# A second feed-forward layer by a seven-product form of Strassen's algorithm, in a kernel bound by TensorE

## The chip, the cores and the metric

The kernel runs on one core of a Trainium2 chip. The metric is the device time of one execution in microseconds, and lower is better. Each run of a kernel lies beside runs of the kernel before on the same chip.

## The reference

Attention with projected keys and values (64 rows for 1,024 tokens), followed by a two-layer feed-forward network. Cut to what matters:

```python
# q, k, v: [8, 8, 1024, 64]   E, F: [64, 1024]
k_proj = einsum('ks,bhsd->bhkd', E, k);  v_proj = einsum('ks,bhsd->bhkd', F, v)
scores = q @ k_proj.T / sqrt(64);        attn = exp(scores - max)
x      = (attn / attn.sum(-1)) @ v_proj          # -> [8192, 512]
h      = x @ w_in                                # w_in  [512, 2048]
g      = h * sigmoid(1.702 * h)
out    = g @ w_out                               # w_out [2048, 512]
```

## The kernel before

The 8,192 tokens are worked in 16 blocks of 512, two for each of eight batch rows. For each block TensorE does the first layer (64 matmuls of 512 columns) and the second (64 more). Attention work for later blocks (scores, values, sums of exponentials, projections of keys and values) is slipped in between groups of these matmuls, in slots. The order on each engine is fixed by the program.

TensorE's results go to PSUM, which the program uses as eight buffers; the kernel before splits them in two pools:

```python
ps_f = ctx.enter_context(tc.tile_pool(name="ps_f", bufs=4, space=PSUM))   # feed-forward layers, scores, projections
ps_x = ctx.enter_context(tc.tile_pool(name="ps_x", bufs=4, space=PSUM))   # values, sums
```

The second layer and the values with their normalization:

```python
def ffn2(j, n, fcs):                     # token tile n of block j
    ...
    if fcs.start == 0:
        o_ps[n] = f_tile([P, DM])
    for fc in fcs:
        nc.tensor.matmul(o_ps[n], gts[j][:, fc, n * P:(n + 1) * P], w_out_sb[:, fc, :],
                         start=(fc == 0), stop=(fc == FC - 1))
    ...

def sums(h):                             # row sums of exp, then their reciprocals
    ...
    for e in range(2):
        nc.vector.reciprocal(rden[:, e, :], d_ps[e])

def spread(h):                           # reciprocals to DRAM, and back to all partitions
    rdr = dram.tile([HP, 2, TB], F32, name="rdr")
    nc.sync.dma_start(out=rdr, in_=rdens.pop(h)[0:P:32])
    rbc[h] = att.tile([P, HP, TB], F32, name="rbc")
    for e, r in enumerate((LO, HI)):
        nc.sync.dma_start(out=rbc[h][r], in_=rdr[None, :, e, :].to_broadcast([D, HP, TB]))

def values(h, u):
    n_ps = [ps_x.tile([P, TB], F32, name="x_ps") for _ in range(2)]
    eight(n_ps, ...)                     # 8 matmuls per pair of heads
    for i in range(2):                   # waits for the broadcast reciprocals
        nc.vector.tensor_tensor(x_of(h)[:, 2 * u + i, :], n_ps[i], rbc[h][:, 2 * u + i, :], op=ALU.mult)

for b in range(4, B):                    # keys and values of row b; frees the buffers of the next row's loads
    at(2 * b - 4, O + 6, proj(b), kv_out(b))
for j in range(3, NBLK - 1):             # O + n: after part n of block j's second layer; conditions for the first and last blocks cut
    at(j, O + 6 * u, scores(j + 3, u))   # for u in 0, 1
    at(j, O, values(j + 1, 1))
    at(j, O, sums(j + 2), spread(j + 2))
    at(j, O + 6, values(j + 2, 0))
```

The softmax here doesn't subtract the row's maximum and nothing guards it: scores larger than these inputs give would overflow.

## Time and profile before

| | before |
|---|---|
| time, median of 4 runs | 508.68 us (508.45 to 509.11) |
| span of the profiled run | 508.2 us |
| TensorE busy | 501.5 us, 99% |
| VectorE busy | 155.0 us, 31% |

The lines of the profile that carry this are in the prediction below. A line of cost groups reads: source line, engine, operation, output <- inputs, count | busy us, mean ns of one | idle time of the engine just before them and what ended it. A line of the timeline reads: start, duration, engine, line, operation, and in brackets how long the engine had been idle and what it waited for. "SPq" and "POOL ... DMA" lines are issues of transfers.

### The profile page before, as it was taken

What the parts mean: (1) busy time and instruction counts of PE and PEld (TensorE: products, weight loads), DVE (VectorE), ACT (ScalarE), POOL (GpSimd) and SP (SyncE); (2) the same over time, 40 slices, a digit from 0 to 9 for tenths busy, and PEclk for the clock granted to TensorE, in tenths of its full rate; (3) what the DMA queues carried; (4) which work ended last, traced back from release to release, by engine and by line L of the source; (5) the groups of instructions that cost most, each with busy time, mean ns of one, the idle gap of its engine ahead of it and who ended that gap; (6) DMA issues with size and microseconds to landing.
All of it is one profiled execution on the core that took longest, in us unless ns stands there. A gap on an engine that the chain in (4) does not pass through costs nothing.

```text
span 508.2 us, 7066 instructions
## 1 busy us (share of the span) xinstructions
PE 501.5 (99%) x3018; PEld 227.7 (45%) x3018; DVE 155.0 (31%) x207; ACT 262.3 (52%) x427; POOL 80.4 (16%) x100
## 2 busy tenths in 40 slices
PE   7999999999999999999999999999999999999997
PEld 3644445444444444444444444444444444444444
DVE  4503204508151624216161331616224161611000
ACT  1665473655637365572746537374563737244351
POOL 6462250500510510041000510000000000000000
PEclk9999999999999999999999999999999999999999
DMA  9999999999899997599928989190603205050202
GB/s 166 200 190 207 201 152 175 219 215 126 150 211 267 134 230 128 159 131 101 234 47 212 99 121 236 29 227 1 173 0 79 88 8 160 1 166 1 83 1 83
DMA packets 127831, 68.76 MB, mean 135 GB/s; under 512 B 94724, under 2 KB 118660, under 8 KB 125880
## 3 DMA queue, kind: packets, MB, share of 16 engines
q0 software_dynamic: 86496, 29.37, 52.8%
q1 hardware_dynamic: 41224, 38.69, 31.3%
q8 instruction: 23, 0.38, 0.3%
q10 hardware_dynamic: 80, 0.26, 0.2%
q14 instruction: 8, 0.07, 0.0%
HBM read 72.88 MB, written 16.99 MB: 177 GB/s over the span
## 4 chain that ended last, share of the span: by engine, by line
PE 95%; DMA 3%; POOL 1%; DVE 0%; issue 0%; ACT 0%; POOLq 0%
PE f_ps L399 44%; PE f_ps L423 43%; DMA v_sb<-in_v_dram 3%; PE f_ps L169 3%; PE f_ps L258 2%; PE x_ps L258 1%; PE f_ps L415 1%; PE x_ps L296 1%; POOL k_sb L57 0%; POOL v_sb L57 0%; PE x_ps L371 0%; PE x_ps L386 0%; PE f_ps L239 0%; POOL q_even L96 0%; DVE x_sb L358 0%
## 5 line engine op out<-in xcount | busy, mean ns | idle before, releaser
L423 PE MATMUL f_ps<-w_out_sb,gT 128*128 128x512 bf16 x1008 | 226.7, 379 | 0.0
L399 PE MATMUL f_ps<-xT,w_in_sb 128*128 128x512 bf16 (+1 forms) x1032 | 224.3, 377 | 0.0
L401 ACT ACTIVATE gT<-f_ps 128x512 bf16<-128x512 f32 (+1 forms) x258 | 150.4, 594 | 58.4 <-PE f_ps L399 58.0
L399 PEld LDWEIGHTS <-w_in_sb 128*128 128x128 bf16 x1032 | 100.7, 98 | 119.7 <-issue 0.8
L423 PEld LDWEIGHTS <-gT 128*128 128x128 bf16 x1008 | 95.9, 98 | 121.8 <-issue 11.8
L426 ACT COPY o_sb<-f_ps 128x512 f32<-128x512 f32 x63 | 37.0, 587 | 130.7 <-PE f_ps L423 120.9
L331 DVE TENSOR_TENSOR xT<-x_ps,rbc 128x512 bf16<-128x512 f32 x52 | 33.3, 684 | 219.2 <-PE x_ps L258 117.8
L299 DVE RECIPROCAL rden<-x_ps 128x512 f32<-128x512 f32 x26 | 85.3, 3322 | 16.2 <-PE x_ps L296 16.1
L69 POOL DMA_DIRECT2D q_sb<-in_q_dram x48 | 42.1, 901 | 153.3 <-DMA qT<-q_sb 124.1
L277 ACT ACTIVATE expT<-f_ps 128x512 bf16<-128x512 f32 (+1 forms) x54 | 28.5, 580 | 29.4 <-PE f_ps L258 29.3
L277 ACT ACT_TABLE_LOAD x13 | 16.7, 1283 | 4.7 <-PE f_ps L258 4.5
L281 ACT ACT_TABLE_LOAD x14 | 18.0, 1283 | 0.2
L57 POOL DMA_DIRECT2D k_sb<-in_k_dram x10 | 8.5, 847 | 48.0 <-PE f_ps L169 41.9
L169 PE MATMUL f_ps<-k_sb,eft 128*64 128x512 bf16 x56 | 13.4, 382 | 0.0
L169 PE MATMUL f_ps<-v_sb,eft 128*64 128x512 bf16 x56 | 13.4, 382 | 0.0
L217 DVE CAST k_b<-f_ps 64x512 bf16<-64x512 f32 x6 | 4.1, 683 | 27.6 <-PE f_ps L169 27.6
L417 DVE COPY o_sb<-f_ps 128x256 f32<-128x256 f32 (+1 forms) x2 | 0.7, 358 | 37.3 <-issue 36.9
L69 POOL DMA_DIRECT2D q_even<-in_q_dram x12 | 10.5, 898 | 8.1 <-DMA k_sb<-in_k_dram 5.1
L138 PE MATMUL x_ps<-zeros 128*128 128x512 bf16 (+1 forms) x20 | 9.4, 601 | 1.5 <-DVE zeros L115 1.5
L258 PE MATMUL x_ps<-expT,vq 64*32 64x512 bf16 x208 | 10.2, 378 | 0.0
L258 PE MATMUL f_ps<-qT,kt 64*32 64x512 bf16 x200 | 10.2, 386 | 0.0
L57 POOL DMA_DIRECT2D v_sb<-in_v_dram x11 | 9.0, 823 | 2.7 <-DMA q_even<-in_q_dram 2.7
(76 smaller groups left out, 125.5 us busy)
## 6 DMA issues: line engine op xcount, KB each, us to landing
out_dram<-o_sb SPq DMA_DIRECT2D x15, 1024.0 KB
rbc<-rdr SPq DMA_DIRECT2D x26, 512.0 KB
k_sb<-in_k_dram POOLq DMA_DIRECT2D x7, 1024.0 KB, 13.0
v_sb<-in_v_dram POOLq DMA_DIRECT2D x7, 1024.0 KB, 19.2
q_sb<-in_q_dram POOLq DMA_DIRECT2D x48, 128.0 KB, 6.2
w_in_sb<-in_moe_w_in_dram POOLq DMA_DIRECT2D x8, 256.0 KB, 11.4
w_out_sb<-in_moe_w_out_dram POOLq DMA_DIRECT2D x4, 512.0 KB, 11.5
q_even<-in_q_dram POOLq DMA_DIRECT2D x12, 128.0 KB, 15.0
```

What stands on the lines that cost most here:

```text
L57: nc.gpsimd.dma_start(out=dst[b][:, h:h + n, js:js + jn], in_=sv[:, h:h + n, js:js + jn])
L69: nc.gpsimd.dma_start(out=qt[b][:, j], in_=qv[:, j])
L169: nc.tensor.matmul(kvps[b][r], eft(j, slice(e * KP, (e + 1) * KP)), (kt, vt)[e][b][:, :, j, :], start=(j == 0), stop=(j == J - 1))
L258: nc.tensor.matmul(outs[i][r.start + c:r.start + c + w], lhsTs[i][ri, c:c + w], rhss[i][ri], start=True, stop=True)
L277: nc.scalar.activation(expT[h][:, 2 * u + i, ts], s_ps[i], AF.Exp, scale=scale)
L281: nc.scalar.preload_act_table(AF.Gelu_apprx_sigmoid)
L299: nc.vector.reciprocal(rden[:, e, :], d_ps[e])
L331: nc.vector.tensor_tensor(x_of(h)[:, 2 * u + i, :], n_ps[i], rbc[h][:, 2 * u + i, :], op=ALU.mult)
L399: nc.tensor.matmul(h_ps, w_in_sb[:, kc, fc * P:(fc + 1) * P], xT[j][:, kc, ts], start=(kc == 0), stop=(kc == KC - 1))
L401: nc.scalar.activation(gts[j][:, fc, ts], h_ps, AF.Gelu_apprx_sigmoid)
L423: nc.tensor.matmul(o_ps[n], gts[j][:, fc, n * P:(n + 1) * P], w_out_sb[:, fc, :], start=(fc == 0), stop=(fc == FC - 1))
L426: nc.scalar.copy(osb[j][:, n, :], o_ps.pop(n))
```

## The change

The intent is to do the second layer from block 1 on with fewer matmul columns. Both operands are cut in halves (gelus by tokens and by features, weights by features and by output columns). Seven products of half-size operands, with 16 matmuls of 256 columns each, take the place of 64 matmuls of 512 columns. VectorE builds four sums of gelus per block and, once, four sums of weights. Some of the adding of products is done by accumulating several of them in one PSUM bank, some by one ScalarE copy from bank to bank and two VectorE adds. The three banks of the products come out of the pools; values and sums lose theirs and share the first layer's five buffers. The core of the diff:

```diff
-    ps_f = ctx.enter_context(tc.tile_pool(name="ps_f", bufs=4, space=PSUM))
-    ps_x = ctx.enter_context(tc.tile_pool(name="ps_x", bufs=4, space=PSUM))
+    ps_f = ctx.enter_context(tc.tile_pool(name="ps_f", bufs=5, space=PSUM))
+    ps_g = ctx.enter_context(tc.tile_pool(name="ps_g", bufs=1, space=PSUM))
...
     def x_tile():
-        return ps_x.tile([P, TB], F32, name="x_ps")
+        return x_any([P, TB])            # after the opening: a first-layer buffer
... (the same in sums, values and the token tiles; rbc with one buffer for two, xT two for three, gT one for two)
+    def w_sums():                        # once, in block 1
+        tt(tw[:, 0], b12, b11, op=ALU.subtract)
+        tt(tw[:, 2], b22, b12, op=ALU.subtract)
+        tt(tmp, b22, b12, op=ALU.subtract)
+        tt(tmp, tmp, b11, op=ALU.add)
+        tt(tw[:, 3], b21, tmp, op=ALU.subtract)
+        nc.vector.tensor_copy(tw[:, 1], tmp)
+    def g_sums(j, c0, n):                # each block, in three pieces
+        tt(t[0], g[:, lo, THI], g[:, hi, THI], op=ALU.add)
+        tt(t[1], t[0], g[:, lo, TLO], op=ALU.subtract)
+        tt(t[2], g[:, lo, TLO], g[:, lo, THI], op=ALU.subtract)
+        tt(t[3], g[:, hi, TLO], t[1], op=ALU.subtract)
+        bank = {1: 0, 2: 0, 6: 1, 7: 1, 4: 1, 5: 2, 3: 2}      # product -> PSUM bank
+        return [p1a, p1b, p5a, p5b, h(6, 0), p6b, h(2, 0), p2b, h(7, 0), p7b,
+                h(4, 0), p4b, h(3, 0), p3b]
...
+    SLOT = {1: 0, 3: 1, 5: 2, 6: 3, 7: 4, 8: 5, 9: 6, 11: 7}   # part of a product -> slot
```

More of the change, by code (lines that the diff above doesn't have):

```diff
@@ L39 @@
     work = ctx.enter_context(tc.tile_pool(name="work", bufs=2))
-    ps_f = ctx.enter_context(tc.tile_pool(name="ps_f", bufs=4, space=PSUM))
-    ps_x = ctx.enter_context(tc.tile_pool(name="ps_x", bufs=4, space=PSUM))
+    ps_f = ctx.enter_context(tc.tile_pool(name="ps_f", bufs=5, space=PSUM))
+    ps_g = ctx.enter_context(tc.tile_pool(name="ps_g", bufs=1, space=PSUM))
     dram = ctx.enter_context(tc.tile_pool(name="dram", bufs=2, space=bass.MemoryType.DRAM))
     ctx.enter_context(tc.manual_schedule())
-    ef_f = consts.tile([P, S], F32, name="ef_f")
+    ef_f = work.tile([P, JB, DM], F32, name="o_sb")[:, :S // DM].rearrange("p j m -> p (j m)")
     ef_sb = consts.tile([P, S], BF16, name="ef_sb")
@@ L113 @@
     zeros = consts.tile([P, TB], BF16)
-    zeros4 = consts.tile([P, TB], F32)
+    zeros4 = work.tile([P, 2, TB // 2], F32, name="u1_sb", bufs=1).rearrange("p i m -> p (i m)")
     nc.vector.memset(zeros4, 0.0)
@@ L133, in f_tile, with x_any @@
         return ps_f.tile(shape, dt, name="f_ps")
+    opening, g_next = [True], [0]
+    def x_any(shape, dt=F32):
+        if not opening[0]:
+            return f_tile(shape, dt)
+        g_next[0] += 1
+        return ps_g.tile(shape, dt, name=f"g{g_next[0] % 3}_ps")
     def warm(n, f=False, z=zeros):
-        w_ps = f_tile([P, TB]) if f else ps_x.tile([P, TB], F32, name="x_ps")
+        w_ps = f_tile([P, TB]) if f else x_any([P, TB])
         for _ in range(n):
@@ L284, in x_of @@
         if h not in xT:
-            xT[h] = att.tile([P, KC, TB], BF16, name="xT", bufs=3)
+            xT[h] = att.tile([P, KC, TB], BF16, name="xT")
         return xT[h]
@@ L291, in go @@
         def go():
-            d_ps = [ps_x.tile([P, TB], F32, name="x_ps") for _ in range(2)]
+            d_ps = [x_any([P, TB]) for _ in range(2)]
             for p in range(HP):
@@ L306, in go @@
             nc.sync.dma_start(out=rdr, in_=rdens.pop(h)[0:P:32])
-            rbc[h] = att.tile([P, HP, TB], F32, name="rbc")
+            rbc[h] = att.tile([P, HP, TB], F32, name="rbc", bufs=1)
             for e, r in enumerate((LO, HI)):
@@ L314, in go @@
             e = [expT[h][:, 2 * u + i, :] for i in range(2)]
-            d_ps = [ps_x.tile([P, TB], F32, name="x_ps") for _ in range(2)]
+            d_ps = [x_any([P, TB]) for _ in range(2)]
             eight(d_ps, [ones, ones], e)
-            n_ps = [ps_x.tile([P, TB], F32, name="x_ps") for _ in range(2)]
+            n_ps = [x_any([P, TB]) for _ in range(2)]
             eight(n_ps, [vqs[h // NB2 % 2][:, 2 * u + i, :] for i in range(2)], e)
@@ L326, in go @@
         def go():
-            n_ps = [ps_x.tile([P, TB], F32, name="x_ps") for _ in range(2)]
+            n_ps = [x_any([P, TB]) for _ in range(2)]
             eight(n_ps, [vqs[h // NB2 % 2][:, 2 * u + i, :] for i in range(2)],
@@ L341, in sums0 @@
     def sums0(half):
-        d_ps = ps_x.tile([P, HP, 2, 2], F32, name="x_ps")
+        d_ps = x_any([P, HP, 2, 2])
         for p in range(HP):
@@ L350, in tok0 @@
     def tok0(p, a):
-        n_ps = (f_tile if a else lambda s: ps_x.tile(s, F32, name="x_ps"))([P, 2, 2, D])
+        n_ps = (f_tile if a else x_any)([P, 2, 2, D])
         for i in range(2):
@@ L360, in x_tr0 @@
     def x_tr0(p, a, n, cp):
-        n_ps = ps_x.tile([P, 2 * n, P], BF16, name="x_ps")
+        n_ps = x_any([P, 2 * n, P], BF16)
         for t in range(2 * n):
@@ L367, in go @@
         def go():
-            d_ps = ps_x.tile([P, 4, D + 1], F32, name="x_ps")
+            d_ps = x_any([P, 4, D + 1])
             for i in range(2):
@@ L383, in go @@
             x_sb = xs.pop((h, p, half)).rearrange("s (i t) d -> s i (t d)", i=2)
-            n_ps = ps_x.tile([P, 2, P], BF16, name="x_ps")
+            n_ps = x_any([P, 2, P], BF16)
             for i in range(2):
@@ L394, in ffn1 @@
         if j not in gts:
-            gts[j] = work.tile([P, FC, TB], BF16, name="gT")
+            gts[j] = work.tile([P, FC, TB], BF16, name="gT", bufs=1)
         n = ts.stop - ts.start
@@ L407, in ffn2 @@
             osb[j] = work.tile([P, JB, DM], F32, name="o_sb")
-        if j == NBLK - 1 and n == JB - 1:
-            if fcs.start == 0:
-                for m0, m, cp in ((0, 2, nc.vector.tensor_copy), (2, 1, nc.vector.tensor_copy), (3, 1, nc.scalar.copy)):
-                    ms = slice(m0 * DM // 4, (m0 + m) * DM // 4)
-                    l_ps = f_tile([P, m * DM // 4])
-                    for fc in range(FC):
-                        nc.tensor.matmul(l_ps, gts[j][:, fc, n * P:(n + 1) * P], w_out_sb[:, fc, ms],
-                                         start=(fc == 0), stop=(fc == FC - 1))
-                    cp(osb[j][:, n, ms], l_ps)
-                    nc.sync.dma_start(out=ov[:, c * JB + n, ms], in_=osb[j][:, n, ms])
-            return
         if fcs.start == 0:
@@ L426, in ffn2 @@
             nc.scalar.copy(osb[j][:, n, :], o_ps.pop(n))
-            if j == NBLK - 1:
-                nc.sync.dma_start(out=ov[:, c * JB + n, :], in_=osb[j][:, n, :])
-            elif n == JB - 1:
+            if n == JB - 1:
                 nc.sync.dma_start(out=ov[:, c * JB:(c + 1) * JB, :], in_=osb[j])
+    FH, TH, MH = FC // 2, TB // 2, DM // 2
+    FLO, FHI = slice(0, FH), slice(FH, FC)
+    TLO, THI = slice(0, TH), slice(TH, TB)
+    b11, b12 = w_out_sb[:, FLO, :MH], w_out_sb[:, FLO, MH:]
@@ new lines @@
+    b21, b22 = w_out_sb[:, FHI, :MH], w_out_sb[:, FHI, MH:]
+    tw = consts.tile([P, 4, FH, MH], BF16, name="tw")
+    sg = consts.tile([P, 4, FH, TH], BF16, name="sg")
+    def w_sums():
+        tt = nc.vector.tensor_tensor
+        tmp = work.tile([P, JB, DM], F32, name="o_sb").rearrange("p (c x) (d m) -> p (c x d) m", x=1, m=MH)
+        tt(tw[:, 0], b12, b11, op=ALU.subtract)
[4 more added lines that the diff above has]
+        nc.vector.tensor_copy(tw[:, 1], tmp)
@@ new lines, in g_sums, with ffn2_parts, prod, tile_of @@
+    def g_sums(j, c0, n):
+        lo, hi = slice(c0, c0 + n), slice(FH + c0, FH + c0 + n)
+        g, t = gts[j], [sg[:, i, c0:c0 + n] for i in range(4)]
+        tt = nc.vector.tensor_tensor
+        tt(t[0], g[:, lo, THI], g[:, hi, THI], op=ALU.add)
+        tt(t[1], t[0], g[:, lo, TLO], op=ALU.subtract)
+        tt(t[2], g[:, lo, TLO], g[:, lo, THI], op=ALU.subtract)
+        tt(t[3], g[:, hi, TLO], t[1], op=ALU.subtract)
+    def ffn2_parts(j, last=False):
+        b, c = divmod(j, NB2)
+        ov = out[b * S:(b + 1) * S, :].rearrange("(p j) m -> p j m", j=J)[:, c * JB:(c + 1) * JB]
+        o = osb[j] = work.tile([P, JB, DM], F32, name="o_sb")
+        g = gts[j]
+        ops = {
+            1: (g[:, FLO, TLO], b11), 2: (g[:, FHI, TLO], b21), 3: (sg[:, 3], b22),
+            4: (g[:, FHI, THI], tw[:, 3]), 5: (sg[:, 0], tw[:, 0]), 6: (sg[:, 1], tw[:, 1]),
+            7: (sg[:, 2], tw[:, 2])}
+        bank = {1: 0, 2: 0, 6: 1, 7: 1, 4: 1, 5: 2, 3: 2}
+        gb, u = {}, {}
+        def prod(i, tc_, first, final):
+            a, w = ops[i]
+            for k in range(FH):
+                nc.tensor.matmul(gb[bank[i]][:, tc_], a[:, k, tc_ * P:(tc_ + 1) * P], w[:, k],
+                                 start=(first and tc_ == 0 and k == 0), stop=(final and k == FH - 1),
+                                 skip_group_check=True)
+        def tile_of(n):
+            gb[n] = ps_g.tile([P, 2, MH], F32, name=f"g{n}_ps")
+        def p1a():
+            tile_of(0)
+            prod(1, 0, True, False)
+        def p1b():
+            prod(1, 1, True, False)
+            tile_of(1)
+            nc.scalar.copy(gb[1], gb[0])
+        def p5a():
+            tile_of(2)
+            prod(5, 0, True, False)
+        def keep(n):
+            u[n] = work.tile([P, 2, MH], F32, name=f"u{n}_sb", bufs=1)
+            nc.scalar.copy(u[n], gb[n])
+        def p5b():
+            prod(5, 1, True, False)
+            keep(2)
+        def p6b():
+            prod(6, 1, False, False)
+            keep(1)
+        def put(ts, ms):
+            if last:
+                nc.sync.dma_start(out=ov[:, ts, ms], in_=o[:, ts, ms])
+        def p2b():
+            prod(2, 1, False, True)
+            nc.scalar.copy(o[:, 0:2, :MH], gb[0])
+            put(slice(0, 2), slice(0, MH))
+        def p7b():
+            prod(7, 1, False, False)
+            nc.vector.tensor_tensor(o[:, 2:4, MH:], gb[1], u[2], op=ALU.add)
+            put(slice(2, 4), slice(MH, DM))
+        def p4b():
+            prod(4, 1, False, True)
+            nc.scalar.copy(o[:, 2:4, :MH], gb[1])
+            put(slice(2, 4), slice(0, MH))
+        def p3b():
+            prod(3, 1, False, True)
+            nc.vector.tensor_tensor(o[:, 0:2, MH:], gb[2], u[1], op=ALU.add)
+            if last:
+                put(slice(0, 2), slice(MH, DM))
+            else:
+                nc.sync.dma_start(out=ov, in_=o)
+        h = lambda i, tc_: lambda: prod(i, tc_, False, False)
+        return [p1a, p1b, p5a, p5b, h(6, 0), p6b, h(2, 0), p2b, h(7, 0), p7b,
+                h(4, 0), p4b, h(3, 0), p3b]
@@ L477 @@
     at(0, Q + 3, gelu_table)
+    at(1, 0, w_sums)
     for p in range(HP):
@@ L522, in filled @@
             f()
+    SLOT = {1: 0, 3: 1, 5: 2, 6: 3, 7: 4, 8: 5, 9: 6, 11: 7}
+    half_first = [fc for p in range(FH) for fc in (p, FH + p)]
     for j in range(NBLK):
@@ L526 @@
             load(j // NB2 + 2)
-        for i, (half, fc) in enumerate(order if j == 0 else [(None, fc) for fc in range(FC)]):
+        for i, (half, fc) in enumerate(order if j == 0 else [(None, fc) for fc in half_first]):
             ffn1(j, fc, slice(0, TB) if half is None else slice(half * TB // 2, (half + 1) * TB // 2))
+            if j and i in (7, 13, 15):
+                c0 = {7: 0, 13: 4, 15: 7}[i]
+                g_sums(j, c0, (i + 1) // 2 - c0)
             filled(j, i)
-        parts = [(n, range(8 * g, 8 * g + 8)) for n in range(JB) for g in range(2)]
         if j == 0:
+            parts = [(n, range(8 * g, 8 * g + 8)) for n in range(JB) for g in range(2)]
             parts[:6] = [(n, range(4 * g, 4 * g + 4)) for g in range(4) for n in range(3)]
-        for s, (n, fcs) in enumerate(parts):
-            ffn2(j, n, fcs)
-            filled(j, (Q if j == 0 else O) + s)
+            for s, (n, fcs) in enumerate(parts):
+                ffn2(j, n, fcs)
+                filled(j, Q + s)
+            continue
+        if j == 1:
+            opening[0] = False
+            g1_ps = ps_g.tile([P, TB], F32, name="g1_ps")
+            nc.tensor.matmul(g1_ps, zeros[:, :P], zeros, start=True, stop=True)
+        for s, part in enumerate(ffn2_parts(j, j == NBLK - 1)):
+            part()
+            if s in SLOT:
+                filled(j, O + SLOT[s])
     assert not fill, fill
```

## The prediction

> **What bounds the kernel now.** I read the page's busy table first, then the chain that ended last, then the cost groups, and then the timeline of one steady block.
>
> ```profile
> PE 501.5 (99%) x3018; PEld 227.7 (45%) x3018; DVE 155.0 (31%) x207; ACT 262.3 (52%) x427; POOL 80.4 (16%) x100
> PEclk9999999999999999999999999999999999999999
> PE 95%; DMA 3%; POOL 1%; DVE 0%; issue 0%; ACT 0%; POOLq 0%
> L423 PE MATMUL f_ps<-w_out_sb,gT 128*128 128x512 bf16 x1008 | 226.7, 379 | 0.0
> L399 PE MATMUL f_ps<-xT,w_in_sb 128*128 128x512 bf16 (+1 forms) x1032 | 224.3, 377 | 0.0
> L299 DVE RECIPROCAL rden<-x_ps 128x512 f32<-128x512 f32 x26 | 85.3, 3322 | 16.2 <-PE x_ps L296 16.1
> ```
>
> See that TensorE is busy 99% at full clock, is 95% of the chain, and has 0.0 us of idle before both layers. Every microsecond of TensorE streaming is on the path; so will be every wait put before it. VectorE has room on average, but its reciprocals come in pairs of 6.6 us.
>
> The timeline around one second layer (block 10, even), lines picked in order of time:
>
> ```profile
> 344.99 1.89 PE L423 MATMUL f_ps<-w_out_sb,gT 128*128 128x512 bf16 x8
> 345.19 0.60 ACT L401 ACTIVATE gT<-f_ps 128x512 bf16<-128x512 f32 x1 [0.27 <-PE f_ps L399]
> 345.80 1.28 ACT L277 ACT_TABLE_LOAD   x1
> 346.81 0.41 PE L258 MATMUL f_ps<-qT,kt 64*32 64x512 bf16 x8
> 347.03 0.40 PE L258 MATMUL x_ps<-expT,vq 64*32 64x512 bf16 x8
> 347.25 0.40 PE L296 MATMUL x_ps<-expT,ones 64*32 64x512 bf16 x8
> 347.47 1.29 DVE L331 TENSOR_TENSOR xT<-x_ps,rbc 128x512 bf16<-128x512 f32 x2 [10.70 <-PE x_ps L258]
> 347.58 10.53 PE L423 MATMUL f_ps<-w_out_sb,gT 128*128 128x512 bf16 x48
> 348.68 6.56 DVE L299 RECIPROCAL rden<-x_ps 128x512 f32<-128x512 f32 x2
> 362.19 13.98 PE L399 MATMUL f_ps<-xT,w_in_sb 128*128 128x512 bf16 x64
> 365.00 1.29 DVE L331 TENSOR_TENSOR xT<-x_ps,rbc 128x512 bf16<-128x512 f32 x2 [3.42 <-PE f_ps L399]
> 376.00 1.89 PE L423 MATMUL f_ps<-w_out_sb,gT 128*128 128x512 bf16 x8
> ```
>
> See three things. 64 matmuls of 512 columns take 376.00-362.19 = 13.81 us, 215.8 ns each. The attention work of a later block (scores, values, sums) is slipped in for 0.86 us (346.72 to 347.58) and TensorE waits for none of it, because it has four PSUM buffers of its own (x_ps). And the second values product waits for the broadcast reciprocals until 365.00, 9.8 us after the reciprocals end: x_ps holds its results meanwhile and nobody minds.
>
> [...] The last token tile of the kernel before (L415) is a check: 16 matmuls of 256 and 32 of 128 columns, each with its own weight load of 98 ns; 16 x 109.2 + 31 x 55.8 = 3.48 us from first to last start, and the trace has 501.50 to 505.0. So weight loads stay hidden at 256 columns. [...]
>
> **Part by part: TensorE's streaming.** In 15 blocks, 64 matmuls of 512 columns become 7 x 16 = 112 of 256: 64 x 215.8 = 13.81 us against 112 x 109.2 = 12.23. That is 1.58 us a block, **23.7 us** in all: the most that the change can give (7/8 of the columns[...]).
>
> **The additions** (my estimate[...]): per block 4 ops each over 4, 3 and 1 chunks of 256: [...]0.69, 0.56 and 0.29 us, about 6 us, plus two fp32 adds of 0.68 and one ScalarE copy of 0.59 more. VectorE goes from 155 to some 275 us (54%): not a bound on average. Weight sums once, about 10.5 us of VectorE at block 1's start.
>
> **What is moved is the dear part: PSUM.** The four x_ps buffers go. Three banks belong to the products, and scores, values, sums and the first layer now share five. The built program's order shows what each takes over. In a steady block (4 to 12), with t=0 at product 1:
> - Products 1a, 1b end at 1.75. Scores start 1.84, values 2.06, sums want 2.28. The second sums tile takes the buffer of the first values tile, so it waits for that VectorE multiply: earliest start 2.06+0.44 = 2.50 (the trace has 0.44 from matmul to multiply), end 3.18; VectorE ends its last sums chunk about 2.3 (last gelu ends 0.80, then 4 short ops behind the 3-chunk piece), just in time. TensorE goes on with product 5 at 3.25+0.33 = 3.58 instead of 2.61: **0.97 us lost.**
> - Products 5, 6, 2, 7 end at 3.58+4x1.744 = 10.56. The reciprocals run 3.9 to 10.5, then VectorE adds product 7 (10.76 to 11.45), and product 4 in the same bank must wait for it: 11.52 where the slipped-in work ends at 11.24 (odd blocks: 0.28 lost; in even blocks a projection of 1.85 us hides it).
> - End 11.52+3.49 = 15.0 against 13.81+0.86+0.68 = 15.35 before: gain 0.34 odd, 0.62 even. For blocks 5 to 12: **-3.9 us.**
> - The reciprocals land about 10.5+9.8 = 20.3; the first-layer tile that reuses their buffers comes at 15.0+7 or 9 x 0.863 = 21 to 23: no stall, one or two us to spare.
>
> **The rest, each worked the same way:**
> - Blocks 13 to 15 have little slipped in, but the product 7 add then stands bare before product 4 (0.9 us), and the tail's last transfer grows from 64 to 256 KB behind a 0.7 us add: -1.4 in sum.
> - Opening and block 0: three buffers for four; the fourth scores tile waits for an exp (0.7), three token tiles for a copy (0.3 each), some 0.4 in the opening: **+2.**
> - Block 1: slots of four 256-column products (0.87 us) stand where 1.73 us stood, but VectorE needs 1.75 us a pair of heads (trace: 0.17+0.42 twice, 0.29 twice): four stalls, 3.7 us, less 1.58: **+2.1.**
> - Block 2: a scores tile waits for an exp which now stands behind a PSUM copy and a 1.28 us table load (1.6), and another for a values multiply whose reciprocals took 18.6 us to land at this time (97.9 to 116.5, the DMA rows full): some 4; less gain: **+4.**
> - Block 3: 2.2 + 0.5 of the same exp waits: **+1.3.** Block 4: a first-layer tile waits for block 3's reciprocals (17 us to land in the trace: 144.1 to 161.1): up to 3.5, say 2: **+1.6** after the 0.4 gain.
>
> Sum: -3.9 -1.4 +2 +2.1 +4 +1.3 +1.6 = +5.7 on 508.5: **514 us.** The waits (some 29 us) give back a little more than the 23.7 gained.
>
> **Rivals.**
> - *Streaming decides*: waits are short or fall into gaps, 508.5-23.7 plus 1.5 of tail: 486. For it: 0.0 us of TensorE waiting before. Against: x_ps, which made that so, is gone[...].
> - *Weight loads show*: [...] Against: L415 hides 98 ns loads even at 128 columns.
> - *VectorE becomes the bound*: [...]
> - *The reciprocals' transfer*: if it takes 3 us longer than 9.8 in steady blocks, each first layer stalls 1 to 2 us: 525. Against: transfers thin out after 150 us.
>
> **Range and chances.** Waits certain by order (0.97 nine times, exps, bare adds, tail) make some 17 us, so 502 is hard to beat; the DMA waits of blocks 2 and 4 and block 1's chain carry 12 of uncertain size. Range **504 to 523**, best guess 514. Faster than 498.4 needs nearly all waits gone: 0.11. Slower than 518.7 needs slow adds or late transfers: 0.21. Within 2%: 0.68.
>
> **What would show it.** Right: TensorE busy falls to about 480 us with over 20 us idle; matmuls of products 109 ns apart; the wait list names VectorE's values multiply before the sums line in most blocks at about 1 us, VectorE's add before product 4, ScalarE's exp and VectorE in blocks 1 to 3; bf16 adds of 0.6 to 0.7 us at 1024 elements. Wrong: product matmuls at 120 ns or more, adds above 1 us, or TensorE idle under 10 us.

## The result, and the profile after

The changed kernel is correct and takes **530.67 us** (median of 4 runs, 527.62 to 532.22), against 508.68 us. The ratio is 1.042 (95% interval 1.038 to 1.046). A ratio here is the mean time of one kernel's runs over that of the other's of the same rounds, so it is not quite the ratio of the medians quoted. The kernel became slower, and slower than the range of the prediction allowed.

From the page of the changed kernel: busy times, the granted clock in 40 slices, the chain of waits by engine, and the cost groups of the first layer (L407) and of one of the products (L474):

```profile
PE 487.2 (92%) x3672; PEld 298.5 (57%) x3707; DVE 266.8 (51%) x421; ACT 274.3 (52%) x442; POOL 81.0 (15%) x100
PEclk9999999999999997999999999999999999999999
PE 69%; DMA 17%; DVE 10%; issue 2%; ACT 1%; SPq 1%; POOL 1%; DVEq 0%; POOLq 0%; ACTq 0%
L407 PE MATMUL f_ps<-xT,w_in_sb 128*128 128x512 bf16 (+1 forms) x1001 | 226.8, 382 | 15.2 <-DVE xT L339 13.6
L474 PE MATMUL g_ps<-tw,gT 128*128 128x256 bf16 x240 | 28.7, 273 | 3.8 <-DVE o_sb L517 3.8
```

TensorE is busy 14 us less, but in a span 19 us longer. The chain, 95% TensorE before, is now 17% transfers and 10% VectorE. And the first layer, which nobody changed, has 15.2 us of idle before it, where it had none. The list of TensorE's waits (total, times, longest, in us) says for what:

```profile
PE f_ps L407 <- DVE xT L339: 13.6, 4, 5.1
PE f_ps L304 <- DVE xT L339: 5.3, 9, 0.6
PE f_ps L266 <- ACT expT L285: 4.0, 3, 1.9
PE g_ps L474 <- DVE o_sb L517: 3.8, 8, 0.8
```

The second to fourth lines are the waits that the prediction names (sums behind a values multiply, exps, the add of product 7). The first is not: four first-layer tiles wait for a values multiply, up to 5.1 us each. The timeline of the changed kernel around one of them (block 8 into block 9), with the issue of the next row's keys and values (L57), of the broadcast (L317), the multiply (L339) and the first layer:

```profile
313.73 0.88 POOL L57 DMA_DIRECT2D k_sb<-in_k_dram  x1 [2.54 <-PE f_ps L177]
314.60 0.89 POOL L57 DMA_DIRECT2D v_sb<-in_v_dram  x1
314.75 2.17 SPq L317 DMA_DIRECT2D rbc<-rdr  x2
...
327.49 1.29 DVE L339 TENSOR_TENSOR xT<-f_ps,rbc 128x512 bf16<-128x512 f32 x2 [12.40 <-DMA rbc<-rdr]
328.23 2.29 PE L407 MATMUL f_ps<-xT,w_in_sb 128*128 128x512 bf16 x5 [4.60 <-DVE xT L339]
```

The same place in the kernel before (L309 is the broadcast, L331 the multiply):

```profile
296.96 1.26 SPq L309 DMA_DIRECT2D rbc<-rdr  x2
...
300.08 0.88 POOL L57 DMA_DIRECT2D k_sb<-in_k_dram  x1 [8.77 <-PE f_ps L169]
...
305.00 1.29 DVE L331 TENSOR_TENSOR xT<-x_ps,rbc 128x512 bf16<-128x512 f32 x2 [3.57 <-DMA rbc<-rdr]
```

Before, the broadcast (1 MB in two transfers) goes out 3.1 us ahead of the load of the keys, and the multiply begins 9.9 us after the reciprocals end (295.06). After, 2 MB of keys and values are issued just ahead of the broadcast; the multiply begins 16.4 us after the reciprocals (311.12), the tile that it should free is wanted after 12.5, and TensorE stands still for 4.60 us.

The stall has a second price. Busy time in three stretches of the changed kernel, each of 36 first-layer matmuls right after a stall (of 5.05, 2.09 and 4.60 us; one matmul record of the second is missing, but its 36 weight loads are there); the columns are length, busy us and count of TensorE, weight loads, VectorE, ScalarE and GpSimd, granted clock (the profile's figure, 1.00 for TensorE's full speed), and two of the transfers:

```profile
200.47:210.41 9.94, 9.89 (x36) 4.02 (x36) 4.59 (x8) 4.78 (x8) 0.00 (x0) 0.78 0.63 169
264.19:271.95 7.76, 7.71 (x35) 3.52 (x36) 4.59 (x8) 4.78 (x8) 0.00 (x0) 1.00 1.19 277
328.23:337.45 9.22, 9.16 (x36) 3.85 (x36) 4.60 (x8) 4.78 (x8) 0.00 (x0) 0.84 0.69 184
```

After the two long stalls the granted clock is 0.78 and 0.84 and the same work takes some 2.2 and 1.5 us longer than after the short one (9.94 and 9.22 us less 7.76).

Where the time went, block by block (from first layer to first layer, in us more than in the kernel before; three experiments of the next section stand beside it):

| block | changed | loads held back | buffers shared, no products | last version |
|---|---|---|---|---|
| opening | -1.5 | -1.6 | 0.0 | -1.3 |
| 0 | +1.8 | +1.8 | +1.8 | +1.0 |
| 1 | +2.3 | +2.5 | +0.1 | -0.5 |
| 2 | +2.1 | +2.3 | +5.5 | +0.7 |
| 3 | +1.3 | +2.9 | +1.6 | -0.7 |
| 4 | +1.4 | -0.1 | +1.1 | -1.4 |
| **5** | **+7.1** | -0.3 | +1.1 | -0.7 |
| 6, 8, 10, each | -0.6 | -0.6 | +1.1 | -1.6 |
| **7** | **+2.0** | -0.3 | +1.1 | -0.7 |
| **9** | **+5.9** | -0.2 | +1.1 | -0.4 |
| 11, 12, each | -0.3 | -0.3 | +1.1 | -1.1, -1.4 |
| 13 to 15, to TensorE's last matmul, sum | -2.0 | -2.0 | +0.1 | -5.1 |
| after the last matmul | +1.3 | +1.3 | +0.9 | +1.2 |

Blocks 5, 7 and 9 are the three that follow an even block with a projection and a new load of keys and values. The opening (until block 0 starts) differs by up to 1.6 us between runs of kernels whose opening is the same, and means nothing here.

### The profile page after: what moved, and what is told of

Same layout as the page of the kernel before. It is cut to its first block, busy times and chain, and to the rows that moved or that the text cites. A ratio compares the mean times of both kernels' runs of the same rounds, so it can differ in the third digit from the quotient of the medians.

```text
span 527.6 us, 8672 instructions
## 1 busy us (share of the span) xinstructions
PE 487.2 (92%) x3672; PEld 298.5 (57%) x3707; DVE 266.8 (51%) x421; ACT 274.3 (52%) x442; POOL 81.0 (15%) x100
## 4 chain that ended last, share of the span: by engine, by line
PE 69%; DMA 17%; DVE 10%; issue 2%; ACT 1%; SPq 1%; POOL 1%; DVEq 0%; POOLq 0%; ACTq 0%
PE f_ps L407 33%; PE g_ps L474 28%; DMA rbc<-rdr 11%; DMA rdr<-rden 3%; DVE rden L307 2%; PE f_ps L419 2%; DVE xT L339 2%; DMA kt<-k_b 2%; PE f_ps L266 2%; DMA q_even<-in_q_dram 2%; DVE o_sb L517 1%; PE f_ps L304 1%; PE f_ps L177 1%; DVE x_sb L386 1%; SPq L317 1%
## 5 line engine op out<-in xcount | busy, mean ns | idle before, releaser
L407 PE MATMUL f_ps<-xT,w_in_sb 128*128 128x512 bf16 (+1 forms) x1001 | 226.8, 382 | 15.2 <-DVE xT L339 13.6
L407 PEld LDWEIGHTS <-w_in_sb 128*128 128x128 bf16 x1032 | 101.4, 99 | 133.9 <-issue 20.5
L474 PEld LDWEIGHTS <-sg 128*128 128x128 bf16 x960 | 92.7, 98 | 14.1 <-issue 2.9
L339 DVE TENSOR_TENSOR xT<-f_ps,rbc 128x512 bf16<-128x512 f32 x52 | 33.3, 684 | 115.2 <-DMA rbc<-rdr 102.5
L307 DVE RECIPROCAL rden<-f_ps 128x512 f32<-128x512 f32 x26 | 85.4, 3326 | 3.6 <-PE f_ps L304 3.5
L474 PE MATMUL g_ps<-tw,sg 128*128 128x256 bf16 x720 | 83.8, 273 | 0.0
L474 PEld LDWEIGHTS <-gT 128*128 128x128 bf16 x720 | 69.6, 98 | 20.1 <-issue 9.1
L474 PE MATMUL g_ps<-w_out_sb,gT 128*128 128x256 bf16 x480 | 57.6, 273 | 0.0
L451 DVE TENSOR_TENSOR sg<-gT 128x1024 bf16<-128x1024 bf16 (+2 forms) x45 | 23.0, 511 | 57.4 <-ACT gT L409 57.4
L474 PE MATMUL g_ps<-tw,gT 128*128 128x256 bf16 x240 | 28.7, 273 | 3.8 <-DVE o_sb L517 3.8
L474 PE MATMUL g_ps<-w_out_sb,sg 128*128 128x256 bf16 x240 | 28.7, 273 | 0.0
L452 DVE TENSOR_TENSOR sg<-sg,gT 128x1024 bf16<-128x1024 bf16 (+2 forms) x45 | 23.1, 514 | 1.6
L453 DVE TENSOR_TENSOR sg<-gT 128x1024 bf16<-128x1024 bf16 (+2 forms) x45 | 22.8, 506 | 0.0
## 6 DMA issues: line engine op xcount, KB each, us to landing
w_in_sb<-in_moe_w_in_dram POOLq DMA_DIRECT2D x8, 256.0 KB, 10.6
q_even<-in_q_dram POOLq DMA_DIRECT2D x12, 128.0 KB, 13.9
```

Of the source, the lines that this page charges most:

```text
L407: nc.tensor.matmul(h_ps, w_in_sb[:, kc, fc * P:(fc + 1) * P], xT[j][:, kc, ts], start=(kc == 0), stop=(kc == KC - 1))
L451: tt(t[0], g[:, lo, THI], g[:, hi, THI], op=ALU.add)
L452: tt(t[1], t[0], g[:, lo, TLO], op=ALU.subtract)
L453: tt(t[2], g[:, lo, TLO], g[:, lo, THI], op=ALU.subtract)
L474: nc.tensor.matmul(gb[bank[i]][:, tc_], a[:, k, tc_ * P:(tc_ + 1) * P], w[:, k], start=(first and tc_ == 0 and k == 0), stop=(final and k ...
```

## The experiments

The theory: in even blocks the projection now comes earlier relative to the broadcast of the reciprocals, frees the key and value buffers earlier, and lets 2 MB of loads begin ahead of it. The late broadcast holds the values multiply; that holds a PSUM buffer; and because first layer and values now share buffers, it holds TensorE. Rivals: the broadcast is late for other reasons (query loads that also run later, its one buffer for two), or the stalls come of the shorter products. The trace speaks against the single buffer: the broadcast's issue waits for the landing of the reciprocals in DRAM (26.6 us in 13 times, 4.0 at most), and from block 4 on the multiply that last read the buffer had ended some 8 to 10 us before. (In block 3 it goes out just as that multiply ends, at 153.94, so there the single buffer may have a part. No run gives the buffer back.)

All ten kernels gave correct results. Each lies beside the kernel before on the same chip. Each has one profiled execution, and the waits told of are from it alone; in proj_later (523.42 us), scores_apart (511.92) and early_blocks (503.88) it was the slowest of the four.

| run | median, us | ratio to before (95%) |
|---|---|---|
| late_loads | 514.28 | 1.009 (1.006 to 1.012) |
| proj_later | 518.82 | 1.021 (1.016 to 1.026) |
| before_early_proj | 508.67 | 0.998 (0.996 to 1.001) |
| shared_five | 530.15 | 1.042 (1.041 to 1.044) |
| scores_apart | 509.66 | 1.001 (0.997 to 1.004) |
| p3_first | 504.31 | 0.990 (0.985 to 0.994) |
| gate4 | 500.43 | 0.985 (0.983 to 0.987) |
| early_blocks | 501.69 | 0.987 (0.985 to 0.990) |
| early2 | 496.51 | 0.976 (0.974 to 0.978) |
| early3 | 494.53 | 0.971 (0.969 to 0.973) |

### late_loads: the loads held back

To the changed kernel:

```diff
+    gate = consts.tile([P, 1], F32, name="gate")
...
     # ahead of each load of keys or values of row b, on GpSimd
+    if b >= 5:
+        nc.gpsimd.tensor_copy(gate, osb[2 * b - 6][:, 2, 0:1])   # what product 4 of that block left
```

> The changed kernel, and the key and value loads of blocks 5 to 7 of the batch (2 MB each, read while block 4, 6 and 8 run) are held back by a one-column GpSimd copy that reads what product 4 left in the output tile of blocks 4, 6 and 8, so that they begin after the broadcast of the reciprocals and not just ahead of it. TensorE, VectorE and ScalarE keep their order. Theory A (the loads, released ahead of the broadcast by the projection, fill the queues before it): the broadcast reciprocals of blocks 4, 6 and 8 land within about 11.5 us of the reciprocals' end instead of 16.8, 13.9 and 16.4; the waits of 5.05, 2.09 and 4.60 us before a first-layer tile in blocks 5, 7 and 9 go, and so does the lowered clock after two of them; about 515 us, 15 less than the changed kernel. Theory B (the broadcast is late for other reasons: the query loads that also run later, or the one buffer for the broadcast): the same waits stay; 527 to 531 us. Both (query loads share): waits of 2 to 3 us in all stay, 517 to 521.

Measured: 514.28 us, 16 less than the changed kernel. The first layer's wait for the multiply is down from 13.6 to 0.3 us. Around block 8 (here L321 is the broadcast, L343 the multiply):

```profile
305.37 1.26 SPq L321 DMA_DIRECT2D rbc<-rdr  x2
...
307.76 0.88 POOL L57 DMA_DIRECT2D k_sb<-in_k_dram  x1 [0.33 <-issue]
...
313.44 1.29 DVE L343 TENSOR_TENSOR xT<-f_ps,rbc 128x512 bf16<-128x512 f32 x2 [7.71 <-PE f_ps L411]
```

The multiply now waits for TensorE, and no longer for the broadcast: 11.7 us after the reciprocals (301.77) it is there at the latest. In the profiled execution blocks 5, 7 and 9 are back within 0.3 us of the kernel before (the table above). Theory A holds, and the rival that other causes make it late falls for most of the delay. A part stays with the query loads: the reciprocals' way to DRAM, from the end of the reciprocals to the issue of the broadcast, still takes 3.6 us here, with the issue of query loads going on until 301.87, where it took 1.9 in the kernel before and that issue ended at 291.3.

### proj_later: only the order of release

```diff
-        at(j, O + 6, proj(b), kv_out(b))
+        at(j, O + 7, proj(b), kv_out(b))
```

> The changed kernel with one thing altered: the projection and key and value transposes of blocks 4, 6, 8 and 10 stand one slot later (after product 4, where they stood after product 7), so the next row's loads are released some 3 us later and come behind the broadcast of the reciprocals in the queues, with no wait added anywhere. Theory A (order of release is the cause): the broadcast lands within 11.5 us of the reciprocals in blocks 4, 6 and 8; the waits of 5.05, 2.09 and 4.60 us go; the product-7 add stands bare before product 4 in four more blocks (0.28 us each): 514 to 518 us. Rival (the loads take their share of the queues wherever they start, so only holding them back until the block is over helps): waits of 2 us and more stay in blocks 5, 7 and 9; 522 to 529.

Measured: 518.82 us, 0.8 over the range that theory A gave. Blocks 5 and 7 lose their stalls (+0.7 and -0.3 us against before, from +7.1 and +2.0), block 9 does not (+6.0) in the profiled execution. The other three executions took 517.83 to 519.39 us, 4 to 6 us less, so most of this stall may be in the profiled one alone. Its timeline:

```profile
308.43 2.28 SPq L317 DMA_DIRECT2D rbc<-rdr  x2
309.53 0.88 POOL L57 DMA_DIRECT2D k_sb<-in_k_dram  x1 [5.12 <-PE f_ps L177]
...
319.46 7.84 PE L407 MATMUL f_ps<-xT,w_in_sb 128*128 128x512 bf16 x22 [3.19 <-DVE xT L339]
```

In block 8 the reciprocals took 4.2 us (304.18 to 308.43) to be sent on, beside the query loads, so the broadcast is only 1.1 us ahead of the keys and takes until 318.7. In block 6 it was 2.5 us ahead, and the multiply began 10.6 us after the reciprocals. In block 4, at 1.8 us, it was 12.2 us and TensorE still waited 0.8. So here the order alone removed the stall, or most of it, with a lead of about 2 us, and the one time that the lead was 1 us it did not. Two causes seem to work together, loads released early and a broadcast sent late beside query loads. The first is shown by late_loads and is the larger; the second is read from the timeline, and no run tested it.

### before_early_proj: the same release in the kernel before

```diff
-        at(j, O + 6, proj(b), kv_out(b))
+        at(j, O + 4, proj(b), kv_out(b))
```

> The kernel before, with the projection and the key and value transposes of an even block two slots earlier, so that the key and value loads of the next batch row are released ahead of the broadcast of the reciprocals, as in the changed kernel. Theory A: the broadcast of blocks 4, 6 and 8 lands 14 to 17 us after the reciprocals instead of 9.4 to 9.9, but as the values wait in PSUM buffers of their own TensorE does not wait for them: 508 to 511 us, PE still busy 98 to 99%. Rival (the loads ahead of the broadcast do not delay it): it lands at 9.4 to 10.5 us, and the time is the same.

Measured: 508.67 us. The same place as above, in block 8:

```profile
295.20 0.88 POOL L57 DMA_DIRECT2D k_sb<-in_k_dram  x1 [7.83 <-PE f_ps L169]
295.54 1.26 SPq L309 DMA_DIRECT2D rbc<-rdr  x2
...
306.79 1.29 DVE L331 TENSOR_TENSOR xT<-x_ps,rbc 128x512 bf16<-128x512 f32 x2 [10.23 <-DMA rbc<-rdr]
```

The multiply begins 16.4, 12.7 and 13.2 us after the reciprocals in blocks 4, 6 and 8 (two of them a little under the 14 that was expected), and TensorE doesn't notice: every block is within 0.1 us of the kernel before. So a late broadcast costs nothing by itself. It costs where the buffers that it holds are those that the first layer wants. "TensorE never waited for the broadcast" was true of the kernel before because of its own four buffers, not because the broadcast came in time.

In this run SyncE's broadcast comes 3.0 to 4.6 us later when GpSimd's load of the keys is 0.3 to 2.5 us ahead of it (the kernel before has 11.8, 9.7 and 9.9 us in these blocks).

### shared_five: the buffers without the products

The changed kernel's pools, single buffers and slots in sharing, but the plain second layer in the three banks, and no sums of gelus or weights:

```diff
-            o_ps[n] = f_tile([P, DM])
+            o_ps[n] = f_tile([P, DM]) if j == 0 else ps_g.tile([P, DM], F32, name=f"g{n % 3}_ps")
... (w_sums, g_sums and ffn2_parts gone; parts and slots as in the kernel before)
```

> The changed kernel's PSUM without its products: scores, values, sums and the first layer share five buffers, three more hold the second layer's results, but the second layer is the plain one of 64 matmuls of 512 columns, with no sums of gelus or weights, and slots as in the kernel before. Theory (as the prediction has it: the sharing is the dear part, and by itself costs nearly what the products save): the sums wait of 0.6 to 1 us in nine blocks (6 to 9 us), exp waits in blocks 2 and 3 (2 to 4), block 0 (1.8) and a wait of some us for reciprocals in block 4: 518 to 526 us. Since the broadcast is issued ahead of the key and value loads again (parts of 1.73 us, as before), no waits of 2 us and more in blocks 5, 7 and 9. Rival (the waits come of the shorter products, not of the sharing): below 513 us.

Measured: 530.15 us, 4 us over the range. The theory's direction holds and its size was too small: 1.1 us is lost in each of blocks 4 to 12, and 5.5 us in block 2, where a scores tile waits 2.9 us for a values multiply and the clock is halved for 3.4 us behind it. Two lines of its list of waits:

```profile
PE f_ps L304 <- DVE xT L339: 5.3, 9, 0.6
PE f_ps L266 <- DVE xT L339: 2.9, 1, 2.9
```

The first line is, to the tenth, that of the changed kernel: the sums wait comes of the sharing, not of the products. And blocks 5, 7 and 9 are no worse than their neighbours: with the plain layer's longer parts the broadcast goes out 4.0 us ahead of the keys again (310.68 against 314.72), so that stall needs both the sharing and the shorter products. The new pools cost 21.7 us of 508.5 here, nearly all of the 23.7 that the products save. That includes the single buffers for the broadcast and the gelus, the lost third buffer for xT and a longer tail (+0.9), which this run does not part from the sharing.

### scores_apart and p3_first: the waits of the steady blocks

On top of late_loads, first the scores of three blocks ahead two slots later, then product 3 ahead of product 4:

```diff
-                at(j, O + 6 * u, scores(j + 3, u))
+                at(j, O + (6 if u else 2), scores(j + 3, u))
```
```diff
-                h(4, 0), p4b, h(3, 0), p3b]
+                h(3, 0), p3b, h(4, 0), p4b]        # the output transfer moves to p4b
```

> The kernel with held-back loads, and the first pair of scores of the third block ahead is moved from the slot of values and sums to two slots later, in blocks 3 to 12. Theory: the sums no longer find all five shared PSUM buffers taken by scores, values and gelus: the wait of 0.97 us before the sums in nine blocks (and 0.6 in the last of those) goes, about 8.7 us less than the kernel with held-back loads, some 506 us if that is at 515. Rival (the sums wait is only moved: the values multiplies are late for VectorE's own reasons and the next tile waits instead): a wait of 0.5 to 1 us comes before the scores or the product after; less than 3 us gained.

> The kernel with held-back loads and moved scores, and product 3 before product 4, so that the add of product 7 has 3.5 us before the next product needs its bank. Theory: the waits for that add before product 4 (0.28 us in odd blocks 5 to 11, 0.75 to 0.84 in blocks 13 to 15) go: about 3.6 us less than the kernel with moved scores, some 502 if that is at 506. Rival (the add of product 3, now earlier on VectorE behind the values multiply that waits for the reciprocals, stalls the bank of the next product or the slipped-in work): nothing gained, or a new wait on VectorE's add.

Measured: 509.66 and 504.31 us. The sums wait is gone, and most of the steady blocks gain 0.4 to 0.8 us (block 10: from -0.6 to -1.4 against before). But only 4.6 of the 8.7 us appear in the sum. The time so saved brings TensorE to the reciprocals earlier, and they now come late in block 4 and a little in block 9:

```profile
PE f_ps L411 <- DVE xT L343: 4.6, 3, 3.3
```

Product 3 first does what it should: the wait for the add of product 7 leaves the list, and the gain of 5.4 us is even more than the 3.6 expected, part of it chance: block 1, which the edit doesn't touch, is 1.9 us shorter in its profiled execution than in that of scores_apart, where a halved clock followed a wait there (mean granted clock of the whole execution 0.991, against 0.989 in scores_apart).

### gate4, early_blocks, early2 and early3: blocks 0 to 4

```diff
# gate4, on top of p3_first: the loads of row 4 too
-                if b >= 5:
-                    nc.gpsimd.tensor_copy(gate, osb[2 * b - 6][:, 2, 0:1])
+                if b >= 4:
+                    nc.gpsimd.tensor_copy(gate, osb[max(2 * b - 6, 3)][:, 2, 0:1])
# early_blocks, on top: tw[:, 1] and tw[:, 3] apart, and a scores pair of block 2 later
+    at(1, O, w_sums2)
-        at(2, O, scores(4, u, None, u > 0))
+        at(2, O + 2 * u, scores(4, u, None, u > 0))
# early2: that scores pair back, and the first values of block 2 later
-        at(2, O + 2 * u, scores(4, u, None, u > 0))
-        at(2, O + 3 * u, values(3, u))
+        at(2, O, scores(4, u, None, u > 0))
+        at(2, O + (3 if u else 5), values(3, u))
# early3: two more
-        at(0, Q + 1, scores(1, u, None, True))
+        at(0, Q + 1, scores(1, u, None, u == 0))
-        at(1, O + 3 + p, x_tr(2, p, 0), x_tr(2, p, 1))
+        at(1, O + 4 + p, x_tr(2, p, 0), x_tr(2, p, 1))
```

> The kernel with product 3 first, and the loads of batch row 4 held back as well (until product 4 of block 3 is copied out), as those of rows 5 to 7 already are. Theory: they are what makes block 3's reciprocals take 15.4 us to arrive; without them they land within 11 us, the wait of 3.04 us in block 4 and the lowered clock behind it (mean 0.95 in that block) go: 4 to 4.5 us less than with product 3 first (504.3), some 500. Rival (other transfers of that time, the query loads and transposes, delay it): the wait stays above 2 us; 503 to 505.

Measured: 500.43 us, as expected. The wait of 3.04 us in block 4 goes (+3.5 to -1.4 us against before), and block 3's multiply begins 10.6 us after the reciprocals where it was 15.3: the same cause a fourth time, for the loads of row 4.

> The kernel with all loads held back, and two edits in blocks 1 and 2: the last two weight sums (two operations of VectorE, 3.5 us) come after block 1's first layer, so that the key projection's cast is not behind them; and the second pair of scores of block 2 stands two slots later. Theory: in block 1 the wait of 1.66 us for the key transpose goes, in block 2 the wait of 1.86 us for an exp and the 1.8 us that 32 matmuls lose behind it at a granted clock of 0.66: 4 to 5.4 us less than with all loads held back, some 495 to 496. Rival (VectorE, now with weight sums beside the gelu sums of block 1, makes product 5 or 6 wait; the exps of block 2 only wait later): a new wait of 1 to 3 us for VectorE in block 1, gain below 2 us.

Measured: 501.69 us, a miss. Block 1 gains 1.8 us as expected (VectorE's cast of the keys no longer stands behind 10.5 us of weight sums). Block 2 loses 5.4 us: with the scores moved behind it, the last tile of the second values takes over a buffer of the first, which wait for block 3's reciprocals, and stands for 5.89 us. It is the very mistake of the change: the order in which buffers come round decides who waits for whom.

> The kernel with the split weight sums, but the second scores of block 2 back in their slot, and the first values of that block three parts later, so that none of the five buffers holds values that wait for block 3's reciprocals while scores want one. Theory: the wait of 5.89 us in block 2 and the exp wait of 1.86 us it replaced both go, and the lowered clock with them: block 2 falls from 41 us to 32.5 to 33.5; in all 494 to 497. Rival (the values find the same late reciprocals at the later slot): a wait of over 1 us before the scores or the projection of block 2; 497 to 500.

> The same with two more edits: in block 0 the second scores pair takes two of the first layer's five buffers (the exp wait of 0.8 us goes), and in block 1 the transposes of normalized values stand one slot later (four waits of 0.26 us for VectorE go). Theory: 1.5 to 2 us less than without these two, some 493 to 495. Rival (block 0's accumulators then wait for an exp; block 2's start waits for the last transpose): within 0.5 us of the kernel without them.

Measured: 496.51 and 494.53 us, both within what was expected (block 2 of early2, at 34.0 us, half a microsecond over it; 2.0 us for the two last edits). In block 2 of early3 a values tile still waits 1.6 us for the multiply of the values before it. Its page:

```profile
PE 479.9 (97%) x3672; PEld 295.2 (60%) x3707; DVE 266.2 (54%) x421; ACT 272.6 (55%) x442; POOL 81.2 (16%) x104
PEclk9999999999999999999999999999999999999999
L411 PE MATMUL f_ps<-xT,w_in_sb 128*128 128x512 bf16 (+1 forms) x1001 | 222.2, 377 | 2.8 <-DVE xT L343 1.1
```

TensorE is busy 21.6 us less than before in a span 15.1 us shorter, and the first layer's idle time is down to 2.8 us from 15.2. This version beats both kernels, by 2.9% and about 36 us.

### The clock after a wait

One wait occurs in the changed kernel and in p3_first alike: 1.86 us for an exp in block 2. The 32 matmuls of 256 columns that follow it, in the changed kernel and then in p3_first:

```profile
110.96 3.67 PE L474 MATMUL g_ps<-tw,sg 128*128 128x256 bf16 x32
```
```profile
111.13 5.33 PE L478 MATMUL g_ps<-tw,sg 128*128 128x256 bf16 x32
```

The same wait was followed by a granted clock of 1.00 once and of 0.69 (110.80 to 116.30) the other time, at a price of 1.7 us. In these traces, up to the last matmul, a halved clock lasts 3.41 or 6.83 us and, within a run, begins whole multiples of 3.41 us apart (in the changed kernel at 198.08 and 327.79, in late_loads at 110.75 and 144.88). With each trace cut into windows of that length, the wait in p3_first falls into one window, 108.08 to 111.49, and the clock is halved in the next:

```profile
108.08:111.49 3.41, 1.55 (x29) 0.67 (x29) 0.31 (x2) 3.19 (x5) 0.00 (x0) 1.00 1.22 243
111.49:114.91 3.42, 3.42 (x19) 2.42 (x17) 0.00 (x0) 1.19 (x3) 0.87 (x1) 0.50 1.34 207
```

In the changed kernel the same wait is split between two windows, 0.6 and 1.3 us, and the clock stays at 1.00; so it does there after the wait of 2.09 us, split into 0.8 and 1.3. So where the wait falls is chance, but what followed was alike in all twelve traces: from 12 us on, each full-clock window with 1.86 us or more of idle TensorE (1.86 in p3_first and late_loads) was followed by a halved one, and none with 1.82 us or less was (1.82 in proj_later). This is read off the traces; no experiment varied it alone.

## Why the prediction was wrong

**Which step failed.** "The reciprocals land about 10.5+9.8 = 20.3; the first-layer tile that reuses their buffers comes at 15.0+7 or 9 x 0.863 = 21 to 23: no stall, one or two us to spare." The path was right, up to the tile and the buffer, and so was the spare: TensorE came to the tile 12.5 us after the reciprocals in block 8. The 9.8 us was wrong. It was read from one block of the kernel before (where it is 9.4 to 11.8 us from block 4 on; the line it was read from names TensorE as what came last, but the blocks where the transfer is named give 9.4 to 9.9 too), taken for a property of the transfer, and moved into a program in which the projection frees the loads' buffers ahead of the broadcast. In blocks 4, 6 and 8 of the changed kernel it was 16.8, 13.9 and 16.4 us; in the odd blocks, with no new loads, 9.4 to 10.1. The stalls (11.7 us in blocks 5, 7 and 9) and the lowered clock behind two of them (3.6) make 15 of the 17 us by which the result exceeds the prediction.

**The rival that came true was named and turned down.** "The reciprocals' transfer: if it takes 3 us longer than 9.8 in steady blocks, each first layer stalls 1 to 2 us: 525. Against: transfers thin out after 150 us." The thinning is an average over the stretch. The slot in which the broadcast runs is exactly the one in which a load of 2 MB begins, and what begins first had changed places. The order of those two issues could have been worked out from the slots beforehand.

**What held.** With the loads held back the changed kernel takes 514.28 us, where the prediction says 514 (4.7 us above the kernel before of its own round, where it says 5.7). The sum of all other terms came near, but by balance: the profiled execution has +2.9 us for block 3 where +1.3 was said (two halved windows, in blocks 2 and 3, are in its time), and -0.1 for block 4 where +1.6 was said; the terms below were off too. The products run 109 ns a matmul, 16 in 1.74 to 1.75 us, as the last token tile of the kernel before did (L415: starts 109 ns apart at 256 columns, 56 at 128). VectorE's bf16 sums take 0.69, 0.56 and 0.28 us, where the author's estimate, which the trace before could not show, was 0.69, 0.56 and 0.29. The sums wait came in all nine blocks and had its size: in block 10 product 5 starts 3.59 us after product 1 (369.92 against 366.33), where 3.58 was said. The steady blocks end within 0.1 us of the walk (-0.27 odd, -0.61 even, against -0.34 and -0.62). The add of product 7 costs its 0.28 us, and 0.75 to 0.84 in the last blocks.

**What was mis-sized.** Blocks 5 to 12 were put at -3.9 and come to -3.1 with the loads held back: block 12 was counted as an even block, but has no projection to hide the add of product 7. Blocks 13 to 15 with the tail were put at -1.4 and came to -0.7. Block 2 was put at +4 and came to +2.1. Opening and block 0 were put at +2: block 0 took +1.8, and the opening varied by as much of itself. Block 4 was put at +1.6 and came to +1.4, with a stall of 1.87 us for block 3's reciprocals where some 2 was said.

**What the prediction called dear.** "The additions" cost little and "what is moved" nearly everything: shared_five shows 21.7 us for the new pools without the products, against some 29 us of waits of all kinds, adds and tail among them, in the prediction's sum.

**Left open.** How the lateness divides between the key and value loads and the query loads. In block 8 the way to DRAM was 1.7 us longer beside query loads, and holding back the keys and values took off at least 4.7 of the 6.5 us. No run moved the query loads alone.

## What to carry to other kernels

A private set of buffers hides how late its data comes, so before taking it away, list what its occupants wait for, and ask of each latency whether the change itself moves what runs beside it. A transfer time read from a trace belongs to the order of issues of that program (here the broadcast took 9.4 to 11.8 us in the kernel before, from block 4 on, and 12.7 to 16.8 in the changed kernel and before_early_proj with a load of 1 or 2 MB issued 0.1 to 2.5 us before it); when a change moves the instruction that frees a load's buffer, work out anew which transfer goes first. And a gain in matmul columns is worth having only after the waits in its way are gone: here the same products cost 22 us as first placed and, with eight small edits of order, saved 15.
